# Scores of split head pairs: K and Q loaded and split once, each head on its own half of the rows

## The chip, the cores and the metric

One core of one Trainium2 chip. The metric is the device time of one launch in microseconds (us).

## The reference

Four batches, eight heads, 768 positions, head dimension 64, all float32. Sliding-window attention with sinks (window 128, 4 sink positions), then a two-layer feed-forward part over the 3072 tokens:

```python
scores = (q @ k.T) / sqrt(64)
keep = (pos_k < n_sink) | ((pos_q - pos_k >= 0) & (pos_q - pos_k < window))
a = softmax(where(keep, scores, -1e9))
x = concat_heads(a @ v)                  # 3072 x 512
h = x @ w_in                             # 512 -> 2048
out = (h * clip(h + 3, 0, 6) / 6) @ w_out
```

The matrices `w_in` and `w_out` arrive as 8-byte numbers and are turned into float32 on the chip.

## The kernel before

**Number format.** TensorE takes float32 either as it is, in two passes per product, or as `fp32r`, a shorter float that it takes in one pass. To keep accuracy in one-pass products the kernel splits an operand into a high part (rounded to `fp32r`) and a low part (the rest) and adds three or four products of parts. So every factor of the feed-forward part is a couple of tiles: `xh`/`xl`, `wih`/`wil`, `gh`/`g`, `woh`/`wol`.

**Work items.** Attention runs over 48 pairs `s`: a unit (256 positions of a batch) and two heads side by side in the 128 partitions, head 0 in rows 0 to 63 and head 1 in rows 64 to 127. Pairs 0 to 11 are plain: unsplit float32, scores by 64-row products (line 607), transposes on TensorE (712), `av` products that fill 64 columns of the array each (786). Pairs 12 to 47 are split. Of these 12 to 15 are near (a unit's first 256 positions, scores of 128 and of 256 columns), and 16 to 47 are far (scores of 272 columns in both of the two tiles `t`). Four pairs make a unit of the feed-forward part: `F` (`ffn1`, line 859, 12 products of 256 columns per half) and `G` (`ffn2`, line 892, 6 products of 512 columns per half), 12 units of 8 steps.

**Scores of a split pair, before.** `A_far` loads K and Q twice, so that each head's 64 rows stand in both halves of the partitions (tiles `kd` and `qd`, the two heads side by side in the free dimension). `B_k` makes the high part over all of `kt` and then overwrites rows 64 to 127 with the low part; `B_q` makes a full high and a full low tile. A product over 128 rows then adds two products of parts at once, so that one score tile of one head takes two products: high Q against (high K over low K), and low Q against the same. `C_score` does two heads by two products for each `t` (line 610): eight products per far pair.

**After the scores.** DVE adds the mask and takes the row minimum (620), ACT takes the exponential (637), DVE and ACT normalise, the transposed probabilities go through a buffer in device memory, POOL cuts them to shape (757), and `E_av` multiplies them with the split V (806; three or four of each head's products use 64 columns of weights, the others 128), adds the sinks (810), and DVE writes `tmp` and the split `x` (`a`, `b`, `y`, `xh`, `xl`).

**Order.** Each engine's order is fixed when the program is written. `all_tasks` lists each task with its engine, an assumed cost, what it comes after, a due number and the buffers it takes and gives; `in_order` lets time run in this model and picks for each free engine the ready task that is due first; `do` issues them in that order. On TensorE it places filler products (`keep_busy`, tile `idle`, line 357) where nothing is ready in the first `QUIET` = 34.8 us of its plan. `MARGIN` is the time a TensorE task is planned to start after a producer on another engine is done, `GIVEN` that after which a buffer counts as free. The last task of the program, `O11.1`, writes the last 128x512 result out of the accumulator in two halves, one on ACT and one on DVE.

Of the kernel before, what the change touches and what calls it, by code (L numbers as in the profile page):

```python
# [31 lines left out]
PART_DUE = (-474.72, 70.36, 106.59, 91.11, 60.03, 88.04, -112.93, 98.23, 72.34, 54.04, 219.53, 258.17, 117.07,  # L32
            108.99, 203.82, 341.65, 140.59, 151.86, 347.73, 543.5, 206.75, 263.79, 966.41, 643.54, 305.36,
            314.5, 678.08, 778.94, 385.32, 681.65, 927.6, 1439.06)
LEAD = {"kq": 204.02, "v": -124.72, "w": -805.13}
QUIET = 34.8
LATE = -387.88
SLOPE = 30.95
GLAG = 28.02
EARLY = {(0, 0): 2230.8, (0, 1): 287.72}  # L40
HOLDS = ("Pt", "pl", "qt")
KQ_HOME = {2: "kd", 3: "qd"}
MARGIN = 0.6
GIVEN = 0.25
WIRE = {"ka": 1.4, "qa": 0.9, "kq": 0.9, "v": 0.7, "w": 1.8, "bl": 0.7, "Q": 0.9, "U": 1.0, "I": 0.9, "J": 0.4}
LAND = {"w": 1.8, "ka": 1.9, "qa": 1.5, "I": 1.6, "J": 1.5, "U": 1.0, "bl": 1.6}
POOL_FREE = 7.5
BOTH = ("m", "c", "n", "kh", "kl", "qh", "ql", "vh", "vl", "bv", "zl", "xl", "wc", "wd", "wh", "wl", "h", "g")
AHEAD = {"load": -1344.45, "kt": -745.39, "v": -782.64, "S": -329.66}
ROOM = {"kq": 3, "dr": 3, "V": 2, "vr": 1, "kd": 1, "qd": 1, "kt": 1, "qt": 1, "bank": 7, "pl": 2, "Pt": 1, "ph": 2, "st": 3, "vs": 1,  # L50
# [3 lines left out]
def all_tasks():  # L54
# [10 lines left out]
    for s in range(PAIRS):  # L65
# [12 lines left out]
        else:  # L78
            hold = ("Pt",)
            add(f"ka{s}", "SP", 1.2, [], d - AHEAD["load"], ("kd",))  # L80
            add(f"qa{s}", "SP", 1.2, [], d - AHEAD["load"] + 0.1, ("qd",))
            add(f"v{s}", "SP", 0.47, [], d - AHEAD["load"] + 0.2, ("V", "vr"))
            add(f"kh{s}", "*", (0.86, 0.5) if far else (0.54, 0.336), [f"ka{s}"], d - AHEAD["kt"], ("kt",))
            add(f"kl{s}", "DVE", 0.905 if far else 0.61, [f"kh{s}"], d - AHEAD["kt"] + 0.1, (), ("kd",))
            add(f"qh{s}", "*", (0.54, 0.336), [f"qa{s}"] + [f"C{NF32 - 1}.0"] * (s == NF32), d - AHEAD["kt"] + 0.2, ("qt",))
            add(f"ql{s}", "DVE", 0.608, [f"qh{s}"], d - AHEAD["kt"] + 0.3, (), ("qd",))
            add(f"vh{s}", "*", (0.41, 0.26) if far else (0.31, 0.2), [f"v{s}"], d - AHEAD["v"])
            add(f"vl{s}", "DVE", 0.45 if far else 0.335, [f"vh{s}"], d - AHEAD["v"] + 0.1, (), ("vr",))
            add(f"C{s}.0", "PE", 0.5 if far else 0.44, [f"kl{s}", f"ql{s}"], d, ("bank", "bank", "Pt"), (), 0.35)
            add(f"C{s}.1", "PE", 0.5 if far else 0.475, [f"C{s}.0"], d + 0.05, ("bank", "bank"), ("kt", "qt"), 0.35)  # L90
# [11 lines left out]
        add(f"c{s}", "DVE", 0.41 if far else 0.2, [f"x{c}" for c in cells] if far else [f"cs{s}"], d + 0.3, lag=0.1)  # L102
# [3 lines left out]
        if far:  # L106
            add(f"T{s}", "DVE", 0.75, [f"n{c}" for c in cells], d + 0.44, ("kq",), ("Pt",))
            add(f"U{s}", "SP", 0.47, [f"T{s}"], d + 0.45, ("dr",), (f"kq@T{s}",))
            add(f"I{s}", "SP", 1.88, [f"U{s}"], d + 0.45, ("kq",), ())
            add(f"J{s}", "SP", 1.41, [f"U{s}"], d + 0.46, ("sd",), (f"dr@U{s}",))  # L110
            add(f"z{s}", "ACT", 0.265, [f"J{s}"], d + 0.62, ("pz",))
            add(f"zl{s}", "DVE", 0.34, [f"z{s}"], d + 0.62, (), ("sd",))
# [28 lines left out]
        if far:  # L141
            b = (s - 16) // 8
            before += [f"zl{s}", f"bv{b}"]
            if s % 8 == 0:
                add(f"bl{b}", "SP", 0.47, [f"c{s - 1}"], d - AHEAD["S"], ("st",) if b else ("st", "vs"))
                add(f"bs{b}", "ACT", 0.55, [f"bl{b}"] + [f"E{s - 1}.1"] * (b > 0), d)
                add(f"bv{b}", "DVE", 0.62, [f"bs{b}"], d + 0.1, (), ("st",))
        add(f"E{s}.1", "PE", 0.64 if far else 0.37, before, d + 0.7, ("bank",) * far, ("ph", "pl", "V") + ("pz",) * far, 0.3)
        add(f"a{s}.0", "*", (0.275, 0.335), [f"E{s}.1"], d + 0.8, ("tmp",))
        add(f"a{s}.1", "*", (0.275, 0.335), [f"E{s}.1", f"a{s}.0"], d + 0.8)  # L150
        add(f"b{s}.0", "DVE", 0.335, [f"a{s}.0"], d + 0.81)
        add(f"b{s}.1", "DVE", 0.335, [f"a{s}.1", f"b{s}.0"], d + 0.82, (), ("bank",))
# [15 lines left out]
    for n in range(UNITS):  # L168
# [25 lines left out]
        for t in range(2):  # L194
            half = (n, t) == (UNITS - 1, 1)
# [13 lines left out]
def in_order(tasks):  # L209
# [23 lines left out]
    while marks:  # L233
# [14 lines left out]
        while moved:  # L248
            moved = False
            for k, e in enumerate(engines):  # L250
# [65 lines left out]
def attn_ffn_kernel(ctx: ExitStack, tc: tile.TileContext, qx, kx, vx, vsx, n_sink, window, w_in, w_out, out):  # L316
# [194 lines left out]
    def A_kq(s, half=0):  # L511
# [7 lines left out]
        both = work.tile([P, 2, 400 if tag == "kd" else UT], F32, tag=tag, name="kq", bufs=3 if tag == "kq" else 1)  # L519
        kr, qr = both[:, 0, 0:UT], both[:, 1, 0:UT]  # L520
# [374 lines left out]
    def ffn_out(tt, pool, state, dst, step=None):  # L895
# [11 lines left out]
        if step != "O":  # L907
            nc.sync.dma_start(out=dst, in_=state[f"e{row}"])
# [224 lines left out]
```

## Time and profile before

| | |
|---|---|
| median of 3 runs | 683.12 us (681.72 to 683.9) |
| the profiled execution, its own time | 681.53 us |
| its span | 679.8 us, granted TensorE clock 0.998 of full speed |
| outside the span | 1.7 us |
| TensorE busy | 666.8 us |
| DVE / ACT / POOL busy | 547.4 / 436.5 / 130.7 us |

Products on TensorE are pipelined: a row's duration covers the way through the array as well, so a duration of 0.28 us can stand in a stream in which a new product starts every 0.12 us. What a product costs is read from the distance between starts. One float32 product in two passes leaves two records; one `fp32r` product leaves one.

### The profile page before, as it was taken

What the parts mean: (1) busy time and instruction counts of PE and PEld (TensorE: products, weight loads), DVE (VectorE), ACT (ScalarE), POOL (GpSimd) and SP (SyncE); (2) the same over time, 40 slices, a digit from 0 to 9 for tenths busy, and PEclk for the clock granted to TensorE, in tenths of its full rate; (3) what the DMA queues carried; (4) which work ended last, traced back from release to release, by engine and by line L of the source; (5) the groups of instructions that cost most, each with busy time, mean ns of one, the idle gap of its engine ahead of it and who ended that gap; (6) DMA issues with size and microseconds to landing.
All of it is one profiled execution on the core that took longest, in us unless ns stands there. A gap on an engine that the chain in (4) does not pass through costs nothing.

```text
span 679.8 us, 13592 instructions
## 1 busy us (share of the span) xinstructions
PE 666.8 (98%) x4522; PEld 601.5 (88%) x4522; DVE 547.4 (81%) x1383; ACT 436.5 (64%) x1118; POOL 130.7 (19%) x288
## 2 busy tenths in 40 slices
PE   9999999999999999999999999999999999999995
PEld 7779987899999989989999999999999999999994
DVE  6999997799999888889889889888998888632221
ACT  6999887667776565666576567567677566522221
POOL 2000000000223322322223224223222322400000
PEclk9999999999999999999999999999999999999999
DMA  7864573357545444354345435345545252200000
GB/s 208 258 186 153 196 227 98 109 155 189 146 123 149 109 126 147 91 148 138 108 111 156 118 99 159 107 115 157 151 113 148 83 140 73 82 1 1 31 1 35
DMA packets 82608, 84.06 MB, mean 124 GB/s; under 512 B 25572, under 2 KB 70884, under 8 KB 82532
## 3 DMA queue, kind: packets, MB, share of 16 engines
q1 hardware_dynamic: 82528, 83.14, 42.4%
q8 instruction: 37, 0.61, 0.4%
q14 instruction: 39, 0.32, 0.2%
q10 hardware_dynamic: 4, 0.00, 0.0%
HBM read 65.80 MB, written 17.30 MB: 122 GB/s over the span
## 4 chain that ended last, share of the span: by engine, by line
PE 78%; DVE 10%; ACT 4%; DMA 4%; issue 2%; SPq 1%; POOL 0%; DVEq 0%; ACTq 0%; POOLq 0%
PE hps L859 33%; PE o L892 33%; PE av L806 5%; PE sp L610 5%; DVE st L458 2%; DVE wt L461 1%; DMA st<-in_w_in_dram 1%; DVE gf L871 1%; DVE g L877 1%; DVE wol L466 1%; DMA st<-in_w_out_dram 1%; ACT Ph L637 1%; PE spt L810 1%; DVE Ph L620 1%; DMA qd<-in_qx_dram 1%
## 5 line engine op out<-in xcount | busy, mean ns | idle before, releaser
L859 PE MATMUL hps<-xh,wih 128*128 128x256 f32 x768 | 218.4, 284 | 2.9 <-DVE tmp L841 1.7
L859 PE MATMUL hps<-xh,wil 128*128 128x256 f32 x768 | 217.2, 283 | 0.0
L859 PE MATMUL hps<-xl,wih 128*128 128x256 f32 x768 | 216.4, 282 | 0.0
L859 PEld LDWEIGHTS hps<-xh,wih 128*128 128x128 f32 x768 | 144.9, 189 | 8.2 <-issue 3.1
L892 PE MATMUL o<-woh,gh 128*128 128x512 f32 x384 | 151.8, 395 | 0.0
L892 PE MATMUL o<-woh,g 128*128 128x512 f32 x384 | 151.4, 394 | 0.0
L892 PE MATMUL o<-wol,gh 128*128 128x512 f32 x384 | 151.2, 394 | 0.0
L859 PEld LDWEIGHTS hps<-xl,wih 128*128 128x128 f32 x768 | 144.8, 189 | 3.2
L859 PEld LDWEIGHTS hps<-xh,wil 128*128 128x128 f32 x768 | 144.7, 188 | 0.0
L868 ACT ACTIVATE gf<-hps,three 128x512 f32<-128x512 f32 x96 | 65.8, 686 | 87.9 <-PE hps L859 87.7
L757 POOL TENSOR_SCALAR_AFFINE_SELECT ph<-pq 128x256 fp32r<-128x256 f32 x128 | 62.9, 511 | 298.1 <-ACT pq L306 180.4
L871 DVE SCALAR_TENSOR_TENSOR gf<-gf,hps 128x512 f32<-128x512 f32 x96 | 65.6, 684 | 58.8 <-ACT gf L868 57.9
L892 PEld LDWEIGHTS o<-woh,g 128*128 128x128 f32 x384 | 72.2, 188 | 17.1
L892 PEld LDWEIGHTS o<-woh,gh 128*128 128x128 f32 x384 | 72.3, 188 | 11.7 <-issue 0.3
L892 PEld LDWEIGHTS o<-wol,gh 128*128 128x128 f32 x384 | 72.3, 188 | 11.7
L877 DVE TENSOR_TENSOR g<-gf,gh 128x512 fp32r<-128x512 f32 x96 | 68.2, 710 | 13.1 <-ACT gh L306 12.2
L306 ACT ACTIVATE gh<-gf 128x512 fp32r<-128x512 f32 x81 | 51.1, 630 | 30.9 <-DVE gf L871 28.9
L637 ACT ACTIVATE Pt<-Pt,nb 128x144 f32<-128x144 f32 (+2 forms) x144 | 59.0, 411 | 17.4 <-DVE Pt L628 16.6
L757 POOL TENSOR_SCALAR_AFFINE_SELECT pl<-pq 128x256 fp32r<-128x256 f32 x128 | 62.6, 508 | 12.0 <-DVE pq L739 11.8
L620 DVE CUSTOM_DVE_ANT_0 Pt<-sp,m_t 128x272 f32<-128x272 f32 x128 | 50.9, 436 | 3.8 <-PE sp L610 3.7
L610 PE MATMUL sp<-kt,qt 128*128 128x272 f32 (+2 forms) x288 | 43.7, 287 | 0.0
L610 PEld LDWEIGHTS sp<-kt,qt 128*128 128x128 f32 x288 | 40.0, 188 | 2.0 <-ACT Pt L637 0.2
(110 smaller groups left out, 978.3 us busy)
## 6 DMA issues: line engine op xcount, KB each, us to landing
kd<-in_kx_dram SPq DMA_DIRECT2D x64, 200.0 KB, 3.5
qd<-in_qx_dram SPq DMA_DIRECT2D x72, 128.0 KB, 3.3
dt<-tb SPq DMA_DIRECT2D x32, 288.0 KB, 2.2
st<-in_w_in_dram SPq DMA_DIRECT2D x16, 512.0 KB, 4.9
st<-in_w_out_dram SPq DMA_DIRECT2D x16, 512.0 KB, 4.6
pd<-dt SPq DMA_DIRECT2D x128, 64.0 KB, 2.1
out_dram<-ost SPq DMA_DIRECT2D x24, 256.0 KB, 2.6
vr<-in_vx_dram SPq DMA_DIRECT2D x32, 192.0 KB, 2.7
```

What stands on the lines that cost most here:

```text
L306: nc.scalar.mul(out=out, in_=src, mul=scale)
L458: nc.vector.scalar_tensor_tensor(out=low, in0=high, scalar=-2 ** 31, in1=low, op0=ALU.bitwise_and, op1=ALU.bitwise_or)
L610: nc.tensor.matmul(out=sp[g][:, 0:w], lhsT=d["qt"][:, i, g, ts], rhs=d["kt"][:, g, ks], start=(i == 0), stop=(i == 1))
L620: nc.vector.tensor_tensor_reduce(out=cell(s, g, t, 0, w), in0=sp[g][:, 0:w], in1=m[:, 0:w], scale=-SCALE, scalar=3.0e38, op0=ALU.add, op1= ...
L637: nc.scalar.activation(out=blk, in_=blk, func=AF.Exp, scale=-1.0, bias=d["nb"][:, i:i + 1], accum_out=d["sm"][:, i:i + 1])
L757: nc.gpsimd.affine_select(out=out, in_=d[f"pq{h}"][:, i].bitcast(F32), pattern=[[0, 2], [step, P]], base=0, channel_multiplier=-step, comp ...
L806: nc.tensor.matmul(out=o, lhsT=l, rhs=r, start=j == 0, stop=j == len(seq) - 1)
L859: nc.tensor.matmul(out=hp[:, half, :], lhsT=l, rhs=r, start=(j == 0 and not (early and half)), stop=(j == n - 1 and not (early and half == ...
L868: nc.scalar.activation(out=gf, in_=hp, func=AF.Relu, bias=three, scale=1.0)
L871: nc.vector.scalar_tensor_tensor(out=gf, in0=gf, scalar=6.0, in1=hp, op0=ALU.min, op1=ALU.mult)
L877: nc.vector.tensor_tensor(out=g, in0=gf, in1=gh.bitcast(F32), op=ALU.subtract)
L892: nc.tensor.matmul(out=acc, lhsT=l[:, f, ts_], rhs=r[i][:, f, :], start=(i == 0 and f == 0 and j == 0), stop=(i == NFP - 1 and f == 1 and ...
```

## The change

A split pair's K and Q are loaded once, as they lie (head 0 in rows 0 to 63, head 1 in rows 64 to 127), into one tile `kd` with two buffers; `qd` is gone. High and low parts of both are full tiles of half the former width: 400 instead of 800 columns for K, 256 instead of 512 for Q. A score tile now takes, for each head, three products over that head's 64 rows: high by high, high by low, low by high (low by low is left out). They are issued head by head, so that the products of the two heads, which use different halves of the rows of the array, follow each other as a couple: three couples per `t` in place of four products.

The planner's numbers change throughout (due numbers, leads, `KQ_HOME`, costs of the changed tasks and of some others). New in the planner is `SLACK` = 0.8: past 45 us of its plan a TensorE task is planned 0.8 us later behind a producer on another engine, and a `bank` of the accumulator counts as free 0.8 us later. The last result is written out whole, on ACT.

```diff
-EARLY = {(0, 0): 2230.8, (0, 1): 287.72}
+EARLY = {(0, 0): 1777.99, (0, 1): -175.55}
...
+SLACK = 0.8
+SETTLED = 45.0
...
-            add(f"ka{s}", "SP", 1.2, [], d - AHEAD["load"], ("kd",))
-            add(f"qa{s}", "SP", 1.2, [], d - AHEAD["load"] + 0.1, ("qd",))
+            add(f"ka{s}", "SP", 0.95, [], d - AHEAD["load"], ("kd",))
...
-            add(f"O{n}.{t}", "ACT", 0.307 if half else 0.581, [f"G{n}.7.{t}"], -50, ("st",), ("bank",))
-            if half:
-                add(f"O{n}.2", "DVE", 0.3, [f"G{n}.7.1"], -50)
-            add(f"Q{n}.{t}", "SP", 0.47, [f"O{n}.{t}"] + [f"O{n}.2"] * half, -50, (), ("st",))
+            add(f"O{n}.{t}", "ACT", 0.581, [f"G{n}.7.{t}"], -50, ("st",), ("bank",))
+            add(f"Q{n}.{t}", "SP", 0.47, [f"O{n}.{t}"], -50, (), ("st",))
...
+                slack = SLACK if now > SETTLED else 0.0
                 if gives:
-                    heapq.heappush(freed, (end + GIVEN, count, gives))
-                    heapq.heappush(marks, end + GIVEN)
+                    back = end + GIVEN + slack * ("bank" in gives)
+                    heapq.heappush(freed, (back, count, gives))
+                    heapq.heappush(marks, back)
...
-                    apart = 0.0 if tasks[nxt][0] == e else lag + MARGIN * (tasks[nxt][0] == "PE")
+                    apart = 0.0 if tasks[nxt][0] == e else lag + (MARGIN + slack) * (tasks[nxt][0] == "PE")
...
-    def A_far(s, which):
+    def A_far(s):
         b, u, p = pus[s]
-        w, src = (ncol(u), kx) if which == "k" else (UT, qx)
-        t = work.tile([P, 2, 400 if which == "k" else UT], F32, name=f"{which}d", bufs=1)
-        for half in ROWS:
-            nc.sync.dma_start(out=t[half, :, 0:w], in_=src[b, u, p, :, 0:w].rearrange("(h d) c -> d h c", h=2))
-        st_[s][f"{which}r"] = t
+        w = ncol(u)
+        t = work.tile([P, 400 + UT], F32, tag="kd", name="kd", bufs=2)
+        nc.sync.dma_start(out=t[:, 0:w], in_=kx[b, u, p, :, 0:w])
+        nc.sync.dma_start(out=t[:, 400:], in_=qx[b, u, p])
+        st_[s].update(kr=t[:, 0:w], qr=t[:, 400:])
...
-            copy_r(nc, e, d["kt"][:, :, 0:w], d["kr"][:, :, 0:w])
-        else:
-            low = d["kt"][ROWS[1], :, 0:w]
-            nc.vector.tensor_tensor(out=low, in0=d["kr"][ROWS[1], :, 0:w], in1=low.bitcast(F32), op=ALU.subtract)
+            copy_r(nc, e, d["kt"][:, 0, 0:w], d["kr"])
+        else:
+            nc.vector.tensor_tensor(out=d["kt"][:, 1, 0:w], in0=d["kr"], in1=d["kt"][:, 0, 0:w].bitcast(F32), op=ALU.subtract)
...
-            d["qt"] = work.tile([P, 2, 2, UT], F32R, name="qt", bufs=1)
+            d["qt"] = work.tile([P, 2, UT], F32R, name="qt", bufs=1)
...
-            for g in range(2):
-                if plain(s):
-                    gs = slice(D * g, D * (g + 1))
-                    nc.tensor.matmul(out=sp[g][:, 0:w], lhsT=d["qr"][gs, ts], rhs=d["kr"][gs, ks], start=True, stop=True)
-                    continue
-                for i in range(2):
-                    nc.tensor.matmul(out=sp[g][:, 0:w], lhsT=d["qt"][:, i, g, ts], rhs=d["kt"][:, g, ks],
-                                     start=(i == 0), stop=(i == 1))
+            if plain(s):
+                terms = ((d["qr"], d["kr"]),)
+            else:
+                terms = [(d["qt"][:, i], d["kt"][:, j]) for i, j in ((0, 0), (0, 1), (1, 0))]
+            for j, (l, r) in enumerate(terms):
+                for g in range(2):
+                    nc.tensor.matmul(out=sp[g][:, 0:w], lhsT=l[ROWS[g], ts], rhs=r[ROWS[g], ks],
+                                     start=j == 0, stop=j == len(terms) - 1)
```

What the planner makes of it shows in the order on TensorE, first in the middle of the program, at a far pair's scores (`sp`) with the `av` products of an earlier pair and feed-forward products (`hps`) around them. Before:

```order
L806 MATMUL av<-ph,VS 128x128
L810 MATMUL spt<-pz,vs 128x256
L610 MATMUL sp<-kt,qt 128x272 x4
L859 MATMUL hps<-xh_4332,wih_108 128x256
L859 MATMUL hps<-xl_4333,wih_108 128x256
L859 MATMUL hps<-xh_4332,wil_116 128x256
L859 MATMUL hps<-xh_4448,wih_108 128x256
```

And of the change, around the two score tiles of a far pair:

```order
L859 MATMUL hps<-xh_4868,wil_116 128x256
L610 MATMUL sp<-kt,qt 128x272 x6
L806 MATMUL av<-ph,VS 128x256
L806 MATMUL av<-ph,VS 128x128
L806 MATMUL av<-pl,VS 64x128 x2
L806 MATMUL av<-pl,VS 64x256
L806 MATMUL av<-ph,VS 128x128
L610 MATMUL sp<-kt,qt 128x272 x6
L859 MATMUL hps<-xh_4353,wih_108 128x256
```

Each score tile is six products of 64 rows instead of four of 128 rows, with products over all 128 rows ahead of them and behind them. Over the program the 36 split pairs make 52 such uninterrupted stretches of 64-row products: 20 pairs have both score tiles in one stretch, 16 have them in two.

The second place is the start of the program on TensorE, from the scores of the fourth or fifth plain pair (`sp<-kq`) to the first feed-forward products, with the filler products `idle` between. Before:

```order
L357 MATMUL idle<-rel 128x128 x2
L712 MATMUL pt<-ident_r,Ph 128x128 x6
L357 MATMUL idle<-rel 128x128
L607 MATMUL sp<-kq 128x128 x2
L607 MATMUL sp<-kq 128x256 x2
L357 MATMUL idle<-rel 128x128 x3
L786 MATMUL av<-pf,VF 64x256 x2
L786 MATMUL av<-pf,VF 64x128 x2
L357 MATMUL idle<-rel 128x128 x2
L712 MATMUL pt<-ident_r,Ph 128x128 x6
L357 MATMUL idle<-rel 128x128 x4
L859 MATMUL hps<-xh_304,wih_104 128x256
```

And of the change:

```order
L358 MATMUL idle<-rel 128x128 x4
L786 MATMUL av<-pf,VF 64x256 x2
L786 MATMUL av<-pf,VF 64x128 x2
L358 MATMUL idle<-rel 128x128 x2
L712 MATMUL pt<-ident_r,Ph 128x128 x6
L358 MATMUL idle<-rel 128x128 x2
L610 MATMUL sp<-kq 128x128 x2
L610 MATMUL sp<-kq 128x256 x2
L859 MATMUL hps<-xh_315,wih_104 128x256
L859 MATMUL hps<-xl_316,wih_104 128x256
L859 MATMUL hps<-xh_315,wil_112 128x256
L786 MATMUL av<-pf,VF 64x256 x2
```

The first feed-forward products now stand ahead of the second pair's `av` products, with 20 instead of 24 filler products ahead of them; over the whole start there are 37 filler products instead of 32.

## Rows read from the trace of the kernel before

**Rows 1.** Profile page: the span, and each engine's busy time.

```profile
span 679.8 us, 13592 instructions
PE 666.8 (98%) x4522; PEld 601.5 (88%) x4522; DVE 547.4 (81%) x1383; ACT 436.5 (64%) x1118; POOL 130.7 (19%) x288
```

**Rows 2.** Windows: stretch, length, busy of PE, PEld, DVE, ACT, POOL, clock, DMA.

```profile
34.00:68.00 34.00, 33.48 (x240) 28.29 (x239) 33.58 (x98) 33.64 (x92) 1.77 (x5) 1.00 0.56 170
306.00:340.00 34.00, 34.00 (x239) 31.33 (x239) 30.52 (x79) 20.73 (x53) 7.87 (x16) 1.00 0.44 123
```

**Rows 3.** Waits of PE, whole span: us in total, times, longest.

```profile
PE hps L859 <- DVE tmp L841: 1.7, 2, 1.2
...
PE hps L859 <- ACT pf L306: 1.2, 1, 1.2
```

**Rows 4.** Timeline of PE, a far pair's scores: start, length, instruction.

```profile
402.63 0.39 PE L892 MATMUL o<-woh,g 128*128 128x512 f32 x1
402.86 1.16 PE L610 MATMUL sp<-kt,qt 128*128 128x272 f32 x8
403.86 0.40 PE L892 MATMUL o<-woh,gh 128*128 128x512 f32 x1
```

**Rows 5.** Timeline of PE, a near pair's scores.

```profile
134.30 1.09 PE L610 MATMUL sp<-kt,qt 128*128 128x128 f32 x8
135.22 0.28 PE L859 MATMUL hps<-xh,wih 128*128 128x256 f32 x1
```

**Rows 6.** Timeline of PE, two plain pairs' 64-row scores and their neighbours.

```profile
33.09 0.82 PE L712 MATMUL pt<-ident_r,Ph 128*128 128x128 f32 x6
33.74 0.39 PE L357 MATMUL idle<-rel 128*128 128x128 f32 x2
34.06 0.49 PE L607 MATMUL sp<-kq 64*128 64x128 f32 x4
34.48 0.39 PE L859 MATMUL hps<-xh,wih 128*128 128x256 f32 x1
34.70 0.27 PE L859 MATMUL hps<-xl,wih 128*128 128x256 f32 x1
34.82 0.28 PE L859 MATMUL hps<-xh,wil 128*128 128x256 f32 x1
...
38.39 0.93 PE L607 MATMUL sp<-kq 64*128 64x128 f32 x8
39.24 0.89 PE L786 MATMUL av<-pf,VF 128*64 128x256 f32 x8
```

**Rows 7.** Timeline of PE, a far pair's products with V.

```profile
409.52 0.34 PE L806 MATMUL av<-ph,VS 128*128 128x256 f32 x2
409.69 0.40 PE L806 MATMUL av<-pl,VS 128*64 128x128 f32 x3
409.93 0.45 PE L806 MATMUL av<-ph,VS 128*128 128x128 f32 x3
...
410.69 0.40 PE L892 MATMUL o<-woh,gh 128*128 128x512 f32 x1
```

**Rows 8.** Groups by line, DVE, low parts: busy us, mean ns; then idle before.

```profile
L563 DVE TENSOR_TENSOR kt<-kd,kt 64x800 fp32r<-64x800 f32 (+1 forms) x36 | 34.8, 966 | 1.1
L571 DVE TENSOR_TENSOR qt<-qd,qt 128x512 fp32r<-128x512 f32 x36 | 25.0, 696 | 1.2 <-ACT qt L306 0.6
L554 DVE TENSOR_TENSOR VS<-vr,VS 128x384 fp32r<-128x384 f32 (+1 forms) x36 | 19.3, 537 | 0.5 <-ACT VS L306 0.4
L826 DVE TENSOR_TENSOR xl<-tmp,xh 128x256 fp32r<-128x256 f32 x36 | 16.6, 462 | 2.6 <-ACT xh L306 1.8
```

**Rows 9.** Timelines of ACT and DVE, the last results written out.

```profile
670.58 0.60 ACT L904 ACTIVATE ost<-o 128x512 f32<-128x512 f32 x1 [2.03 <-PE o L892]
671.97 0.38 ACT L904 ACTIVATE ost<-o 128x256 f32<-128x256 f32 x1 [0.80 <-PE o L892]
...
672.39 0.42 DVE L906 TENSOR_SCALAR ost<-o 128x256 f32<-128x256 f32 x1 [3.12 <-ACT ost L904]
```

More of the change, by code (lines that the diff above doesn't have):

```diff
@@ L101, in all_tasks @@
             add(f"cs{s}", "POOL", 0.22, [f"x{c}" for c in cells], d + 0.29)
-        add(f"c{s}", "DVE", 0.41 if far else 0.2, [f"x{c}" for c in cells] if far else [f"cs{s}"], d + 0.3, lag=0.1)
+        add(f"c{s}", "DVE", 0.4 if far else 0.12, [f"x{c}" for c in cells] if far else [f"cs{s}"], d + 0.3, lag=0.1)
         for c in cells:
@@ L110, in all_tasks @@
             add(f"J{s}", "SP", 1.41, [f"U{s}"], d + 0.46, ("sd",), (f"dr@U{s}",))
-            add(f"z{s}", "ACT", 0.265, [f"J{s}"], d + 0.62, ("pz",))
-            add(f"zl{s}", "DVE", 0.34, [f"z{s}"], d + 0.62, (), ("sd",))
+            add(f"z{s}", "ACT", 0.31, [f"J{s}"], d + 0.62, ("pz",))
+            add(f"zl{s}", "DVE", 0.41, [f"z{s}"], d + 0.62, (), ("sd",))
         for h in range(2):
@@ L145, in all_tasks @@
                 add(f"bl{b}", "SP", 0.47, [f"c{s - 1}"], d - AHEAD["S"], ("st",) if b else ("st", "vs"))
-                add(f"bs{b}", "ACT", 0.55, [f"bl{b}"] + [f"E{s - 1}.1"] * (b > 0), d)
+                add(f"bs{b}", "ACT", 0.64, [f"bl{b}"] + [f"E{s - 1}.1"] * (b > 0), d)
                 add(f"bv{b}", "DVE", 0.62, [f"bs{b}"], d + 0.1, (), ("st",))
         add(f"E{s}.1", "PE", 0.64 if far else 0.37, before, d + 0.7, ("bank",) * far, ("ph", "pl", "V") + ("pz",) * far, 0.3)
[L149 to L152, printed above, removed]
+        add(f"a{s}.0", "*", (0.37, 0.4), [f"E{s}.1"], d + 0.8, ("tmp",))
+        add(f"a{s}.1", "*", (0.37, 0.4), [f"E{s}.1", f"a{s}.0"], d + 0.8)
+        add(f"b{s}.0", "DVE", 0.4, [f"a{s}.0"], d + 0.81)
+        add(f"b{s}.1", "DVE", 0.4, [f"a{s}.1", f"b{s}.0"], d + 0.82, (), ("bank",))
         if far:
@@ L194, in all_tasks @@
         for t in range(2):
-            half = (n, t) == (UNITS - 1, 1)
-            add(f"O{n}.{t}", "ACT", 0.307 if half else 0.581, [f"G{n}.7.{t}"], -50, ("st",), ("bank",))
-            if half:
-                add(f"O{n}.2", "DVE", 0.3, [f"G{n}.7.1"], -50)
-            add(f"Q{n}.{t}", "SP", 0.47, [f"O{n}.{t}"] + [f"O{n}.2"] * half, -50, (), ("st",))
+            add(f"O{n}.{t}", "ACT", 0.581, [f"G{n}.7.{t}"], -50, ("st",), ("bank",))
+            add(f"Q{n}.{t}", "SP", 0.47, [f"O{n}.{t}"], -50, (), ("st",))
     return tasks
@@ L518, in A_kq @@
         tag = KQ_HOME.get(s, "kq")
-        both = work.tile([P, 2, 400 if tag == "kd" else UT], F32, tag=tag, name="kq", bufs=3 if tag == "kq" else 1)
-        kr, qr = both[:, 0, 0:UT], both[:, 1, 0:UT]
+        both = work.tile([P, 400 + UT if tag == "kd" else 2 * UT], F32, tag=tag, name="kq", bufs=3 if tag == "kq" else 2)
+        kr, qr = both[:, 0:UT], both[:, UT:2 * UT]
         cs = slice(0, UT if s else P)
@@ L895, in ffn_out @@
     def ffn_out(tt, pool, state, dst, step=None):
-        row = min(tt, 1)
         if step != "Q":
-            if f"e{row}" not in state:
-                state[f"e{row}"] = pool.tile([P, DM], F32, tag="st", name="ost", bufs=3)
-            last = step and state["n"] == UNITS - 1 and tt
-            cs = slice(256 * tt - 256, 256 * tt) if last else slice(0, DM)
-            to, src = state[f"e{row}"][:, cs], state[f"o{row}"][:, cs]
-            if tt < 2:
-                nc.scalar.mul(out=to, in_=src, mul=1.0 / 6.0)
-            else:
-                nc.vector.tensor_scalar(out=to, in0=src, scalar1=1.0 / 6.0, scalar2=None, op0=ALU.mult)
+            state[f"e{tt}"] = pool.tile([P, DM], F32, tag="st", name="ost", bufs=3)
+            nc.scalar.mul(out=state[f"e{tt}"], in_=state[f"o{tt}"], mul=1.0 / 6.0)
         if step != "O":
-            nc.sync.dma_start(out=dst, in_=state[f"e{row}"])
+            nc.sync.dma_start(out=dst, in_=state[f"e{tt}"])
     def ffn_steps(n, x, pool, psum_h, psum_o, dsts, tag=None):
@@ L951, in do @@
         elif kind in ("O", "Q"):
-            ffn_out(at[1], work, states[at[0]], dsts(at[0])[min(at[1], 1)], kind)
+            ffn_out(at[1], work, states[at[0]], dsts(at[0])[at[1]], kind)
         else:
             {"mask": lambda: masks(at[0]), "idle": lambda: keep_busy(1), "kq": lambda: A_kq(at[0]), "kb": lambda: A_kq(0, 1), "v": lambda: A_v(at[0]),
-             "ka": lambda: A_far(at[0], "k"), "qa": lambda: A_far(at[0], "q"),
+             "ka": lambda: A_far(at[0]),
              "kh": lambda: B_k(at[0], 0, on), "kl": lambda: B_k(at[0], 1), "qh": lambda: B_q(at[0], 0, on),
```

37 lines of the change are left out of this document (19 added, 18 removed).

## The prediction

> **What bounds the kernel now.** I read the page first: TensorE is busy for 666.8 of 679.8 us, DVE, the next one, for 547.4 [rows 1]. A busy share can deceive where products are pipelined, so the second view was the windows: from 306 to 340 us TensorE is busy for all 34.00 us, at full clock, and DVE (30.52) and ACT (20.73) are not; only early, from 34 to 68 us, are DVE and ACT as full (33.58 and 33.64), with the weights to convert [rows 2]. The third was the waits of TensorE: the feed-forward products waited for DVE twice, 1.7 us together, and for ACT once, 1.2 us [rows 3]; nothing larger stands there. So the time is the sum of what TensorE streams, and a term is worth what it takes or gives in starts of products there. DVE, ACT and the queues count only where they end a wait.
>
> **Edit 1: the score products (TensorE).** Before, a far pair's eight products go from 402.86 to 403.86, 0.125 us from start to start for 272 columns [rows 4]; 32 far pairs make 32.0 us. A near pair's eight take 134.30 to 135.22, 0.92 us [rows 5]: four of 128 and four of 256 columns. At the 0.12 of a 256-column product [rows 6] the latter are 0.48, which leaves 0.44, 0.11 each, for the former; four pairs make 3.7 us.
>
> After, a far pair has six couples of 64-row products. Do the two of a couple run at the same time? Rows of 64-row products there are only of plain pairs, in float32. The eight records from 38.39 to 39.24 are two heads by two passes by 128 and by 256 columns. Transposes of 128 columns start every 0.65/6 = 0.11 us (33.09 to 33.74), so a pass of 256 takes 0.22. One after the other the eight would take 4 x 0.11 + 4 x 0.22 = 1.32 us; as couples, 0.66. The row shows 0.85 [rows 6]: couples, plus 0.19 that I come to below. So I take a couple at the price of one full product: 6 x 0.125 = 0.75 us per far pair, 24.0 for 32; and 3 x 0.11 + 3 x 0.12 = 0.69 per near pair, 2.8 for four. Gain: 32.0 + 3.7 - 24.0 - 2.8 = **8.9 us**.
>
> **Edit 1, second price: changing between 128-row and 64-row products.** The order shows 52 stretches of 64-row products where there were none, each with full products on both sides. What does an entry and a leaving cost? The plain pairs give the upper bound. At 33.74 a filler product, two passes and so 0.22 at the transposes' pace, takes 0.32 before the scores start at 34.06: 0.10 more. The four records to 34.48 are two couples, 0.22, and take 0.42: 0.20 more. The first `hps` product then takes 0.22 to 34.70, the next 0.12: 0.10 more [rows 6]. That is **0.40 us per stretch**, and 52 of them would be 20.8 us, more than twice the gain. The lower bound comes from the products with V: they change between 128 and 64 columns of weights four times per far pair, in `fp32r`, and the whole stretch takes 409.52 to 410.69, 1.17 us [rows 7], for 2,304 columns (1,024 per head, 256 for the sinks), which at the pace of [rows 4] are 1.06. So four changes cost at most 0.11 us, less than a quarter of one plain stretch. The change between a two-pass and a one-pass stream isn't what costs either: transposes and fillers follow one another at 0.11 [rows 6].
>
> The two kinds of rows contradict each other, and neither is the new case: the plain rows have its shape (64 rows, two products at a time) and not its number format; the V rows have its format and a smaller shape, but fill one part of the array alone. I take the lower bound, **0**, for the forecast: what is common to all the costly rows is plain float32 in two passes, and in the one place where this kernel changes shape in the format of the new products nothing is lost. But this is the weakest choice here, and its other end is the first rival.
>
> The Trainium skill speaks against my choice: "TensorEngine Tiling (Array Packing)", section Key Properties, says that changing the tiling mode, not just the tile, drains TensorE. The plain pairs agree with it and the V products, if they count as a change of mode, do not. By the page's rule the sum would be the first rival's, by the V rows it is the forecast's.
>
> **Edit 2: half the splitting and half the loads.** DVE's low parts of K and Q take 966 and 696 ns; at half the width they are nearest to the 537 of a 384-column and the 462 of a 256-column subtraction: 0.66 us less per split pair, some 24 us over 36 pairs; ACT's high parts shrink alike, and each pair has two loads fewer in SP's queue [rows 8]. On the time I cost this at 0. TensorE covers it: where the split pairs run, it streams without a gap while DVE and ACT have idle time [rows 2]. If that cover were gone, the 24 us of DVE would be the most it could give. New behind it: K and Q share one buffer, given back only when both low parts are done, so a late `ql` now holds the next load of K too; with two such buffers that load is a pair ahead, and a wait there is in SP's queue, not on TensorE.
>
> **Edit 3: the roomier plan.** It can only take waits away from TensorE or make new ones. The two on DVE are of the kind it addresses, a TensorE task planned close behind DVE's release of an accumulator bank; at 0.55 and 1.2 us, the plan's extra 0.8 covers the one and most of the other, and DVE's shorter `kl` and `ql` stand ahead of such releases. I take **-1.7 us** [rows 3]; bounds -1.7 and, where the new order makes as many waits as it removes, 0. The wait on ACT lies at the start, where the plan has no slack.
>
> **Edit 4: the start.** Five more filler products (37 against 32), each put where the plan has nothing ready. At 0.22 us each [rows 6] that is **+1.1 us**, if they stand for time in which TensorE really has no work. Below, the 1.2 us wait for ACT before a feed-forward product may go (-1.2), since that product has moved; above, the first such product, now ahead of the second pair's `av`, may wait for its weights with all that is queued behind it: as much again as the wait of before, +2.3.
>
> **Edit 5: the last eviction.** The two halves did not run side by side: ACT's starts at 671.97, DVE's at 672.39 and ends at 672.81. A whole eviction on ACT took 0.60, so it would end at 672.57: **-0.2 us** [rows 9]; what follows (the store) is unchanged.
>
> **Sum.** -8.9 - 1.7 + 1.1 - 0.2 = -9.7 us on the profiled execution's 681.53, which is its span of 679.8 [rows 1] and 1.7 around it: 671.8. The median of the runs shown is 683.12, 1.6 above the profiled one; from it the same sum gives **673.4 us**. With the bounds of edits 3 and 4 and a couple's pace between 0.12 and 0.14 us, the forecast's own range is 669 to 679.
>
> **The rivals.**
> First, the other side: each stretch of 64-row products pays the 0.40 us of the plain ones. For it: both plain stretches of [rows 6], which have the shape of the new products. Against it: [rows 7]. Time: 20.8 us on top of the forecast, 694.2. It decides from 9.7 / 52 = 0.19 us per stretch on.
> Second, half of that, 0.20 us per stretch (the way in or the way out alone): +10.4, 683.8, so nothing gained that can be measured.
> Third, the products are as cheap as I say but the new order makes TensorE wait: accumulator banks are held longer by the plan's own account, and TensorE issues strictly in order, so a feed-forward product that waits for a bank holds all behind it. The nearest rows are the two waits of before, 0.9 us each on average [rows 3]; with one at ten of the far pairs, and those of before not removed, 9 + 1.7 us of the gain go: 684.1; with half as many, 679.6. Against it: the shorter DVE work.
>
> **How the numbers follow.** The runs of before spread over 2.2 us, so about 0.3% is what a measurement can tell from no change: below 681.1 is faster, above 685.2 slower. The forecast has 0.60; the 64-row stretches at full price 0.20; at half price 0.10; the new waits 0.10. The predicted time is the forecast's. Forecast, new waits and half price hold 0.8, from 668 to 686; the full price is left outside. Faster: 0.60 and, of new waits, 0.06; slower: 0.20, and 0.05 of the half price; the rest, 0.09, is no change.
>
> **What would show it.** Edit 1: a far pair's six couples go in 0.75 us and the product ahead and the first behind keep their 0.12 or 0.23 from start to start; if they stretch to 0.22 and 0.33, the first rival is right. The sum of starts over the score line is 27 us against 36. Edit 2: DVE busy near 523 us. Edit 3: no wait of TensorE above 0.5 us past 45 us. Edit 4: TensorE's first feed-forward product waits for a weight tile. Edit 5: the last eviction is one row of 0.60. I am wrong if the 64-row stretches cost more than 0.1 us each, if the two products of a couple don't start together (each pair then takes 1.5 us, 16 us more than now), or if TensorE has gaps where the windows now show none.

## The result and the profile after

The changed kernel took **687.31 us** (median of 4 runs, 686.86 to 687.8); the kernel before, run beside it, took 683.32 (4 runs, 681.72 to 683.9). The ratio is 1.0062, 95% interval 1.0043 to 1.0081: slower by 4.0 us. The forecast was 673.4 with a range of 668 to 686, so both the number and the side were wrong. The profiled execution of the changed kernel took 687.8 us, its span was 686.1, the granted TensorE clock 0.999. The account below goes by the profiled executions, 681.53 and 687.8 us, at granted clocks of 0.998 and 0.999; they lie 6.3 us apart where the medians lie 4.0. That goes with the clock: over the 42 runs beside the experiments the kernel before was granted 0.991 to 0.998 of full speed and took 681.4 to 683.6 us in the six runs at 0.998, 683.6 to 687.5 in the nine at 0.994 or less; the changed kernel had 0.998 or 0.999 in all four.

The profile page of the changed kernel, span, busy time and the group of the new score products:

```profile
span 686.1 us, 13698 instructions
PE 679.1 (99%) x4676; PEld 598.3 (87%) x4676; DVE 517.2 (75%) x1383; ACT 421.2 (61%) x1117; POOL 129.6 (19%) x288
...
L610 PE MATMUL sp<-kt,qt 64*128 64x272 f32 (+2 forms) x432 | 40.7, 308 | 0.0
```

Against [rows 1], DVE lost 30 us and TensorE gained 12.3. So DVE's relief, 517 where 523 was forecast, came, and the kernel is slower all the same: TensorE was the bound and still is. The windows of the changed kernel (columns as in [rows 2]) say the same of the middle of the program:

```profile
306.00:340.00 34.00, 34.00 (x248) 30.16 (x247) 26.95 (x75) 20.31 (x56) 10.54 (x23) 1.00 0.37 110
```

A TensorE that is never idle and yet takes longer must need longer for what it streams. The timeline of PE in the changed kernel, around a far pair whose two score tiles stand in one stretch, shows where:

```profile
406.35 0.28 PE L859 MATMUL hps<-xl,wih 128*128 128x256 f32 x1
406.47 0.28 PE L859 MATMUL hps<-xh,wil 128*128 128x256 f32 x1
406.68 1.02 PE L610 MATMUL sp<-kt,qt 64*128 64x272 f32 x12
407.63 0.50 PE L892 MATMUL o<-woh,gh 128*128 128x512 f32 x1
407.97 0.39 PE L892 MATMUL o<-wol,gh 128*128 128x512 f32 x1
408.20 0.39 PE L892 MATMUL o<-woh,g 128*128 128x512 f32 x1
```

Read the starts, not the durations. The feed-forward product at 406.35 keeps its 0.12 us. The next one, ahead of the scores, takes 0.21: 0.09 more. The twelve 64-row products take 0.95, where six couples at 0.125 are 0.75: so couples they are, plus 0.20. The first product behind takes 0.34, its neighbour 0.23: 0.11 more. That is 0.40 us around one stretch, the figure worked out from the plain pairs in [rows 6], at the same four places. Nothing waits for a semaphore there: this view writes a wait in brackets behind its row, as in [rows 9], and there is none.

One pair is not all 52 stretches. Summed over the trace, the products ahead of the stretches take 4.9 us more than the usual distance for their kind, the stretches themselves 37.0 us where their couples alone would be 26.8, and the first products behind 5.1 us more: 20.2 us, 0.39 per stretch.

The weight loads (PEld) at the same place show what is missing:

```profile
406.35 0.19 PEld L859 LDWEIGHTS hps<-xh,wil 128*128 128x128 f32 x1
406.68 0.80 PEld L610 LDWEIGHTS sp<-kt,qt 64*128 64x128 f32 x12
407.63 0.19 PEld L892 LDWEIGHTS o<-woh,gh 128*128 128x128 f32 x1
```

The weights of the product that starts at 406.47 begin to load at 406.35, when the product ahead of it starts; such a load is hidden. Those of the first 64-row product begin at 406.68, with the product itself, and so do those of the first full product behind, at 407.63. It is the same at all 52 entries and all 52 leavings: the load begins 1 or 2 ns ahead of its own product.

The waits of PE in the changed kernel (us in total, times, longest), all but that of the first filler product for its operand, which POOL writes (1.2 us in both kernels):

```profile
PE av L786 <- ACT pf L307: 0.3, 1, 0.3
PE hps L859 <- DVE wil L467: 0.2, 1, 0.2
PE sp L610 <- ACT pf L307: 0.2, 1, 0.2
```

The waits of [rows 3] are gone, and with them two smaller ones (0.5 and 0.2 us; a third went from 0.3 to 0.2): 3.9 us before, 0.7 now. The end of the program, in the timelines of PE and of ACT in the changed kernel:

```profile
680.72 0.40 PE L892 MATMUL o<-woh,g 128*128 128x512 f32 x1
...
681.15 0.60 ACT L898 ACTIVATE ost<-o 128x512 f32<-128x512 f32 x1 [0.81 <-PE o L892]
```

From the start of the last product to the end of the span it is 686.1 - 680.72 = 5.4 us. I call that the tail. Before, the last product started at 671.54 and the span ended at 679.8: 8.3 us. Its row before:

```profile
671.54 0.40 PE L892 MATMUL o<-woh,g 128*128 128x512 f32 x1
```

So the last product is 9.2 us later, the tail is 2.9 shorter, and the span is 6.3 longer. Two things were to be settled: what makes the stretches dear, and why the tail shrank by 2.9 us where one eviction in place of two was to give 0.2.

### The profile page after: what moved, and what is told of

Read it like the earlier page. It is cut to its first block, busy times and chain, and to the rows that moved or that the text cites. A ratio compares the mean times of both kernels' runs of the same rounds, so it can differ in the third digit from the quotient of the medians.

```text
span 686.1 us, 13698 instructions
## 1 busy us (share of the span) xinstructions
PE 679.1 (99%) x4676; PEld 598.3 (87%) x4676; DVE 517.2 (75%) x1383; ACT 421.2 (61%) x1117; POOL 129.6 (19%) x288
## 4 chain that ended last, share of the span: by engine, by line
PE 85%; DVE 10%; issue 2%; ACT 2%; DMA 1%; POOL 0%; DVEq 0%; POOLq 0%; SPq 0%; ACTq 0%
PE o L892 36%; PE hps L859 35%; PE sp L610 6%; PE av L806 5%; DVE st L459 3%; DVE wt L462 2%; DVE Ph L620 1%; DVE wol L467 1%; DMA st<-in_w_in_dram 1%; PE spt L810 1%; PE idle L358 1%; DVE gf L871 1%; DVE Ph L658 1%; DVE wil L467 1%; DVE g L877 1%
## 5 line engine op out<-in xcount | busy, mean ns | idle before, releaser
L892 PE MATMUL o<-woh,gh 128*128 128x512 f32 x384 | 154.5, 402 | 0.0
L892 PEld LDWEIGHTS o<-wol,gh 128*128 128x128 f32 x384 | 72.3, 188 | 12.3
L307 ACT ACTIVATE gh<-gf 128x512 fp32r<-128x512 f32 x85 | 53.4, 629 | 31.7 <-DVE gf L871 30.6
L307 ACT ACTIVATE kt<-kd 128x400 fp32r<-128x400 f32 (+1 forms) x35 | 18.4, 527 | 41.1 <-PE sp L610 41.1
L610 PE MATMUL sp<-kt,qt 64*128 64x272 f32 (+2 forms) x432 | 40.7, 308 | 0.0
```

Of the source, the lines that this page charges most:

```text
L307: nc.scalar.mul(out=out, in_=src, mul=scale)
L610: nc.tensor.matmul(out=sp[g][:, 0:w], lhsT=l[ROWS[g], ts], rhs=r[ROWS[g], ks], start=j == 0, stop=j == len(terms) - 1)
L892: nc.tensor.matmul(out=acc, lhsT=l[:, f, ts_], rhs=r[i][:, f, :], start=(i == 0 and f == 0 and j == 0), stop=(i == NFP - 1 and f == 1 and ...
```

## The experiments

The letters are those of the expectations. **S**: the stretches of 64-row products cost 0.40 us each at their ends, and this alone makes the kernel slower. **T**: the tail's gain comes from the whole last eviction.

**e1_before_whole_out**: the kernel before, with the last result written out whole.

```diff
-            half = (n, t) == (UNITS - 1, 1)
-            add(f"O{n}.{t}", "ACT", 0.307 if half else 0.581, [f"G{n}.7.{t}"], -50, ("st",), ("bank",))
-            if half:
-                add(f"O{n}.2", "DVE", 0.3, [f"G{n}.7.1"], -50)
...
+            add(f"O{n}.{t}", "ACT", 0.581, [f"G{n}.7.{t}"], -50, ("st",), ("bank",))
...
```

> The kernel before with one part of the change alone: the last result is written out whole on ACT. Theory T (a DVE that still has a piece of the eviction comes late to the end of the program, and the end waits for it): the time from the last product to the end of the span falls from 8.3 to about 5.4 us, so 2.9 us less, about 680.4. Rival (the forecast's step: only the eviction itself gets shorter): 0.2 us less, about 683.1, tail 8.1 us.

680.09 us (11 runs) against 683.46 (22 runs) of the kernel before: ratio 0.9965 (0.9944 to 0.9985). The timeline of PE ends with this row, the span at 677.6:

```profile
671.75 0.40 PE L889 MATMUL o<-woh,g 128*128 128x512 f32 x1
```

The last product stands where it stood (0.2 later), and the tail is 5.9 us instead of 8.3. By itself this speaks for T.

**e2_after_halves**: the changed kernel, with the two halves again (the reverse of the edit above).

> The changed kernel with the last eviction in two halves again, on ACT and DVE. Theory T: 2.9 us more than the changed kernel, about 690.2, with a tail of 8.3 us. Rival: 0.2 us more, about 687.5.

687.99 us (4 runs), 1.0079 (1.006 to 1.0099) of the kernel before. The span is 686.2, and the timelines of PE and of DVE end with:

```profile
680.21 0.40 PE L895 MATMUL o<-woh,g 128*128 128x512 f32 x1
...
681.06 0.42 DVE L909 TENSOR_SCALAR ost<-o 128x256 f32<-128x256 f32 x1 [3.15 <-ACT ost L907]
```

The tail is 6.0 us with both halves in it: 0.6 more than in the changed kernel, not 2.9. T as I had put it falls: a late half on DVE does not by itself make a tail of 8.3 us.

**e3_after_joined**: the changed kernel, with both score tiles of every split pair in one stretch, which makes 36 stretches of 52. The planner takes the joined task as one that asks for four banks, and its order on TensorE differs from the changed kernel's from 129 us on.

```diff
-            add(f"C{s}.0", "PE", 0.4 if far else 0.35, [f"kl{s}", f"ql{s}"], d, ("bank", "bank", "Pt"), (), 0.35)
-            add(f"C{s}.1", "PE", 0.39 if far else 0.37, [f"C{s}.0"], d + 0.05, ("bank", "bank"), ("kt", "qt"), 0.35)
+            add(f"C{s}", "PE", 1.19 if far else 1.12, [f"kl{s}", f"ql{s}"], d, ("bank", "bank", "bank", "bank", "Pt"), ("kt", "qt"), 0.35)
...
```

> The changed kernel with both score tiles of a split pair issued as one task, so 36 stretches of 64-row products instead of 52. Theory S (each stretch costs 0.40 us at its two ends): 16 x 0.40 = 6.4 us less than the changed kernel, about 680.9. Rival P (the ends are hidden, the new plan is what costs): nothing gained, 687 or, since the task takes four banks at once and TensorE waits for them, more.

682.92 us (10 runs), 0.9987 (0.9968 to 1.0005) of the kernel before, 4.4 less than the changed kernel. Sixteen stretches at 0.40 are 6.4. The rest is in the waits of PE, of which these come on top of those of the changed kernel:

```profile
PE av L785 <- DVE Ph L657: 0.5, 1, 0.5
PE av L805 <- ACT ph L306: 0.3, 1, 0.3
...
PE o L891 <- DVE g L876: 0.3, 1, 0.3
...
PE av L805 <- DVE pl L742: 0.3, 1, 0.3
```

They make 1.4 us of the 2.0 that are missing; the other 0.6 I could not assign to single rows. Where a stretch is avoided its price comes back, and new waits of the other order cost part of it. That the four banks make them is not shown: each of these rows waits for an operand.

**e4_full_rows**: the changed kernel in its own order, with products over all 128 rows where the 64-row products stood, four per score tile of a far pair in place of six.

```diff
-                    nc.tensor.matmul(out=sp[g][:, 0:w], lhsT=l[ROWS[g], ts], rhs=r[ROWS[g], ks],
-                                     start=j == 0, stop=j == len(terms) - 1)
+                    if plain(s):
+                        nc.tensor.matmul(out=sp[g][:, 0:w], lhsT=l[ROWS[g], ts], rhs=r[ROWS[g], ks], start=True, stop=True)
+                    elif j < 2:
+                        nc.tensor.matmul(out=sp[g][:, 0:w], lhsT=l[:, ts], rhs=r[:, ks], start=j == 0, stop=j == 1)
```

> The changed kernel in the same order, but each score tile of a split pair takes two products per head over all 128 rows (which adds the two heads together and leaves out low Q by high K, so the scores are not those of the reference) instead of three couples of 64 rows. Theory S: no 64-row stretch in the split pairs, four products of 0.125 us a tile; 47.1 us of stretches and their ends become 35.7, so 11.4 us less than the changed kernel, about 675.9. Rival P (the plan costs, not the ends): within 2 us of 687.

675.48 us (4 runs), 0.9892 (0.9874 to 0.9911) of the kernel before. The timeline of PE around one pair:

```profile
399.50 0.28 PE L861 MATMUL hps<-xh,wil 128*128 128x256 f32 x1
399.62 1.17 PE L613 MATMUL sp<-kt,qt 128*128 128x272 f32 x8
400.62 0.39 PE L894 MATMUL o<-woh,gh 128*128 128x512 f32 x1
400.85 0.39 PE L894 MATMUL o<-wol,gh 128*128 128x512 f32 x1
...
669.28 0.40 PE L894 MATMUL o<-woh,g 128*128 128x512 f32 x1
```

A third more streamed columns per pair (1.00 us instead of 0.75 of content), no ends (0.12 ahead, 0.23 behind), and the last product comes 680.72 - 669.28 = 11.4 us sooner, in the same order with the same plan. With the gain of 8.9 us that is 20.3 over 52 stretches, 0.39 each. That agrees with the 20.2 us counted in the changed kernel's own rows. S holds, and nothing else in the changed kernel is needed to make it slower.

**e5_rows_origin**: the same 64-row products, all on rows 0 to 63, so that the two of a couple can't share the array. It asks whether sharing makes the ends dear or (S1 of the expectation) the 64-row shape itself.

```diff
-                    nc.tensor.matmul(out=sp[g][:, 0:w], lhsT=l[ROWS[g], ts], rhs=r[ROWS[g], ks],
+                    nc.tensor.matmul(out=sp[g][:, 0:w], lhsT=l[ROWS[g if plain(s) else 0], ts], rhs=r[ROWS[g if plain(s) else 0], ks],
```

> The changed kernel with both heads' score products of the split pairs on rows 0 to 63 (head 1 takes head 0's data, so its scores are not those of the reference). The two products of a couple then cannot run at once: 24 + 3 us of products more. Theory S1 (a change between 128-row and 64-row products costs by itself, whichever rows are used): the product ahead of a stretch and the first behind keep their extra 0.09 and 0.10 us, 0.4 us a stretch, time about 714. Rival S2 (it costs because two products share the array): no extra at the ends, about 21 us less, 693.

713.36 us (one run). The timeline of PE around one pair:

```profile
421.77 0.28 PE L859 MATMUL hps<-xh,wil 128*128 128x256 f32 x1
421.98 1.77 PE L610 MATMUL sp<-kt,qt 64*128 64x272 f32 x12
423.68 0.50 PE L892 MATMUL o<-woh,gh 128*128 128x512 f32 x1
424.01 0.39 PE L892 MATMUL o<-wol,gh 128*128 128x512 f32 x1
```

Twelve products one after the other at 0.125 are 1.50 us; the row takes 1.70, again 0.20 more, with 0.21 ahead and 0.33 behind. So two products at a time are not the reason: products of 64 rows between products of 128 rows pay, in `fp32r` as in float32. What inside TensorE takes the time is not shown beyond the loads that do not run ahead.

**e6_v_low_f32**: why, then, did the V products of [rows 7] pay nothing? They were the row on which I had staked the lower bound. Here is the kernel before with the low parts of these products in plain float32; same shape, same place, other format (F: the format decides).

```diff
-            low = [(VS[:, slot, vhi], pl[:, c:c + o1 - o0], acc[0:D, o0:o1]) for slot, c, o0, o1 in ops]
+            low = [(VS[:, slot, vhi].bitcast(F32), pl[:, c:c + o1 - o0].bitcast(F32), acc[0:D, o0:o1]) for slot, c, o0, o1 in ops]
```

> The kernel before, with the 64-column products of V's high part and the low probabilities of the split pairs in plain float32 (two passes at half the rate: 0.47 us of stream per far pair become 1.9, some 46 us more in all). Theory F (a change of shape costs in plain float32 and not in fp32r): each of the four changes per far pair now shows 0.1 to 0.2 us extra at the product ahead and behind, time about 750 or above. Rival G (64 columns that begin at column 0 need no change in either format): starts follow one another at the stream's pace, time about 729.

747.4 us (one run). The timeline of PE, the same piece as [rows 7]:

```profile
453.14 0.34 PE L806 MATMUL av<-ph,VS 128*128 128x256 f32 x2
453.41 1.08 PE L806 MATMUL av<-pl,VS 128*64 128x128 f32 x6
454.42 0.56 PE L806 MATMUL av<-ph,VS 128*128 128x128 f32 x3
454.91 1.08 PE L806 MATMUL av<-pl,VS 128*64 128x128 f32 x6
455.92 0.33 PE L806 MATMUL av<-ph,VS 128*128 128x128 f32 x1
456.09 0.33 PE L810 MATMUL spt<-pz,vs 128*128 128x256 f32 x1
456.26 0.40 PE L892 MATMUL o<-woh,gh 128*128 128x512 f32 x1
```

The rows of the kernel before that [rows 7] leaves out:

```profile
410.22 0.40 PE L806 MATMUL av<-pl,VS 128*64 128x128 f32 x3
410.46 0.22 PE L806 MATMUL av<-ph,VS 128*128 128x128 f32 x1
410.52 0.33 PE L810 MATMUL spt<-pz,vs 128*128 128x256 f32 x1
```

Now the ends are there. The two high products ahead take 0.27 us (0.17 in [rows 7]), the three between the two low groups 0.49 (0.29), the single one behind 0.17 (0.06): 0.10 at each of four ends. A low group, four passes of 128 and two of 256 columns, takes 1.01, where the plain pace (0.11 and 0.22) gives 0.88: another 0.13 in each. All of it went to 3.12 us from 1.17, of which the second passes are 2 x (0.88 - 0.24) = 1.28 and the changes the other 0.67. So `fp32r` products with 64 columns of weights in the array's first columns run between full ones as if nothing changed, and the same shape in float32 does not.

The edit changes the format at each end as well as keeping the shape, so the change of format alone is a rival. The trace of the kernel before has it between full products, float32 transposes among `fp32r` products:

```profile
37.16 0.28 PE L859 MATMUL hps<-xh,wil 128*128 128x256 f32 x1
37.28 0.82 PE L712 MATMUL pt<-ident_r,Ph 128*128 128x128 f32 x6
37.86 0.36 PE L859 MATMUL hps<-xh,wih 128*128 128x256 f32 x1
38.06 0.28 PE L859 MATMUL hps<-xl,wih 128*128 128x256 f32 x1
```

The product ahead keeps its 0.12 us, and the six transposes with the first product behind take 0.78, where 6 x 0.11 and 0.12 are 0.78: nothing extra. In e6, then, the cost needs both, the shape and the format. The V rows were no evidence on products of 64 rows.

**e7_before_slack_whole**: the kernel before, with the planner's `SLACK` and the whole eviction, and its old due numbers.

```diff
+SLACK = 0.8
+SETTLED = 45.0
...
+                    back = end + GIVEN + slack * ("bank" in gives)
...
+                    apart = 0.0 if tasks[nxt][0] == e else lag + (MARGIN + slack) * (tasks[nxt][0] == "PE")
```

> The kernel before with the whole last eviction and with the planner's slack of 0.8 us, its due numbers and costs as they were. If slack takes away the waits of TensorE past 45 us (3.0 us in the kernel with the whole eviction alone): about 677. Rival (the new order makes as many waits elsewhere): 680 or more.

686.96 us (5 runs), 1.0065 (1.0042 to 1.0088) of the kernel before, and 6.9 above e1, from which it differs by the slack alone. The waits of PE, the longest:

```profile
PE hps L860 <- ACT pf L307: 2.1, 1, 2.1
PE hps L860 <- DVE xl L827: 1.3, 1, 1.3
...
PE av L787 <- ACT pf L307: 1.2, 1, 1.2
PE o L893 <- ACT gh L307: 1.1, 1, 1.1
```

All its waits but the first filler's are 8.5 us, in e1 5.0. Of the 3.5 more, 1.8 lie ahead of 45 us, where the slack does not act and both kernels have the same order on TensorE (up to 47.9 us); past 45 us it is 4.9 against 3.2. So slack with the old due numbers takes no waits away and the kernel is slower with it; more than 3 us of the 6.9 are in no wait, and I can't say where they come from.

**e8_plan_full_rows**: the changed kernel's planner numbers, slack and whole eviction, with loads, splitting and score products (and their costs and buffers in the plan) as before.

```diff
-KQ_HOME = {2: "kd", 3: "kd"}
+KQ_HOME = {2: "kd", 3: "qd"}
...
-            add(f"C{s}.0", "PE", 0.4 if far else 0.35, [f"kl{s}", f"ql{s}"], d, ("bank", "bank", "Pt"), (), 0.35)
+            add(f"C{s}.0", "PE", 0.5 if far else 0.44, [f"kl{s}", f"ql{s}"], d, ("bank", "bank", "Pt"), (), 0.35)
```

> The scores, loads and splitting of the kernel before (128-row products, no 64-row stretch in the split pairs) under the changed kernel's planner, due numbers and whole last eviction. Theory S: as the run of full rows on the changed kernel, about 675.5, since what DVE and ACT do more is hidden. Rival D (the 24 us of DVE work that come back end waits of TensorE again): waits of 2 to 4 us, about 678 to 680.

679.48 us (6 runs), 0.9939 (0.9922 to 0.9957) of the kernel before. The last product starts at 672.71, 1.2 us later than before, and the tail is 6.1. The waits of PE are of another kind than those of the changed kernel:

```profile
PE hps L860 <- DVE wil L467: 1.4, 2, 0.8
...
PE pt L713 <- DVE gf L872: 0.8, 1, 0.8
PE av L787 <- ACT pf L307: 0.6, 2, 0.4
```

The rival D of the expectation came true. Against e4, which streams its scores at the same pace but has the short splitting, the last product is 3.4 us later (669.28 there), and the waits without the first filler's are 3.9 us against 0.5: with the full splitting work the numbers don't fit as well. On the profiled executions (680.5 against 681.53) what is gained against before lies in the tail; of the medians' 4.1 us that is not shown.

**e9_mixed_plan**: e8 with the due numbers of the weights (`PART_DUE`), the leads and the numbers of the first feed-forward steps (`EARLY`) of the kernel before.

```diff
-EARLY = {(0, 0): 1777.99, (0, 1): -175.55}
+EARLY = {(0, 0): 2230.8, (0, 1): 287.72}
...
```

> The kernel before with the whole last eviction, the planner's slack and costs of the change and its due numbers for everything but the weights and the first feed-forward steps, which keep those of before. If the waits between 34 and 102 us in the run with all of the new numbers came from the weights' new due numbers: those 3 us go, about 676.5. Rival: the old numbers for the weights clash with the rest, waits of 3 us or more, 680 or above.

680.16 us (5 runs), 0.9941 (0.991 to 0.9972) of the kernel before: not to be told from e8 or e1, and the hoped-for 676.5 did not come. The waits of e8 for weights are gone, and waits took other places (1.4, 1.0 and 0.8 us before the transposes `pt`).

**e10_dve_shift**: the kernel before, with a constant's memset done twelve times on DVE at the start. The end of the program is the same instruction by instruction, both halves included; only DVE's program is eleven instructions longer.

```diff
-    nc.vector.memset(three, 3.0)
+    for _ in range(12):
+        nc.vector.memset(three, 3.0)
```

> The kernel before, halves of the last eviction kept, with 11 more small writes to a constant at the start of DVE's program, so that all that follows stands 11 instructions later there. If the 8.3 us from the last product to the end hang on where DVE's end of program lies in the blocks in which its instructions are fetched: a tail of about 6 us, as in the changed kernel with halves, where DVE's program is 11 rows longer. Rival T (a DVE that is late with its half is what costs): 8.3 us again. The 11 writes themselves are under 1 us and DVE waits there anyway.

681.01 us (one run). The span is 679.3, the timelines of PE and of DVE end with:

```profile
673.28 0.40 PE L893 MATMUL o<-woh,g 128*128 128x512 f32 x1
...
674.13 0.42 DVE L907 TENSOR_SCALAR ost<-o 128x256 f32<-128x256 f32 x1 [3.12 <-ACT ost L905]
```

The tail is 6.0 us, not 8.3, with the same last evictions at the same distances (the DVE half starts 0.85 us behind the last product in both). The last product comes 1.7 us later (the waits are 5.4 us against 3.9), so the run as a whole gains only 0.5.

The trace holds rows that the views leave out, the semaphores and the closing drain of each engine. Counted from the start of the last product, DVE's last semaphore row ends at 5.09 us in the kernel before and its drain begins at 7.40; the end of the span follows 0.9 us behind that. In e6, whose DVE program is that of before, it is 5.09 and 7.41, and the tail is 8.3 as well. In e10 it is 5.02 and 5.11, in e2 5.00 and 5.09. So the 2.3 us are a gap between two neighbouring instructions of DVE, which comes and goes with the length of DVE's program. It costs time only where DVE is last: e3 has such a gap too, from 0.84 to 3.38, but DVE has no half to write there, SP and ACT close after 4.5, and the tail is 5.4. Theory T thus holds for the kernel before, where the half makes DVE late and the gap comes on top; of e1's gain, 2.3 us are owed to this accident. The gap is read from one profile of each kernel. What DVE does in it is not shown, and that stays open.

## Why the prediction was wrong

**Edit 1, the products: right.** A couple costs what one full product costs: 0.95 - 0.20 us over six couples in the changed kernel, 1.50 for twelve single ones in e5. The gain of 8.9 us was there.

**Edit 1, second price: the step that failed.** The prediction had both ends, 0.40 us per stretch and 0, and said: "I take the lower bound, **0**, for the forecast". The stretch costs 0.40 at its four places, 20.2 us in all by the changed kernel's rows and 20.3 by e4. The reason given, "what is common to all the costly rows is plain float32 in two passes", was a coincidence: e5 and the changed kernel itself pay in `fp32r`. The counter-evidence, [rows 7], had the other shape, 64 columns and not 64 rows, and e6 shows that this shape is free in `fp32r` only. Nor could the transposes and fillers of [rows 6] rule out the change of format, as the prediction has it: both stand in float32, and only the rows beside e6 show that change. A row with the new products' own geometry and another format was set aside for a row with their format and another geometry. From the profile of before alone the first rival deserved at least half the chance; it got 0.20.

The Trainium skill's sentence in "TensorEngine Tiling (Array Packing)", section Key Properties, that a change of tiling mode drains TensorE, speaks of the 64-row stretches here, and the trace agrees as far as it goes: 0.40 us per stretch, and no weight load that runs ahead across its ends; a drain itself has no row in the middle of the program. For 64 columns in `fp32r` the trace shows no such cost (at most 0.11 us for four changes, [rows 7]), in float32 it does (0.67 per pair, e6).

**Why not 694.2.** The first rival had the mechanism and its price, and stood 7 us too high. About 5 of these come from the rest of the sum, which it took from the forecast; the other 2 from the medians, since the forecast set out from one that lay 1.6 above the profiled execution, and the changed kernel's lies 0.5 below its own. On the profiled executions, from 681.53 to 687.8, +6.3: the stretches net of the gain, +11.4 (e4); five more fillers, +1.1 as forecast (the distances from a filler row to the next row, summed over the start, grow from 11.4 to 12.6 us without the wait); the waits, -3.2 (3.9 to 0.7), of which the forecast had 1.7 and its bounds another 1.2 at the start; the tail, -2.9 where -0.2 was forecast. That makes +6.4. The forecast's own range adds up to 670 to 679 from its terms, not 669; nothing hangs on it.

**Edits 2 to 5.** Edit 2: half right. The relief is as large as forecast, but its 0 took it as hidden wherever TensorE streams, and e8 against e4 shows 3.4 us of waits that come back under the new plan with the full work (and with the loads and buffers of before). Edit 3: right in size, past 45 us the waits went from 2.4 to 0.7 us and none is above 0.3; e7 and e8 show that this is the plan and the shorter DVE work fitted together, not the slack alone. Edit 4: the fillers as forecast, and the wait for ACT of [rows 3] gone, the lower bound of that term; the feared wait for a weight tile did not appear (the longest is 0.2). Edit 5: the last eviction is one row of 0.60 us as forecast; the halves cost 0.6 (e2), and 2.3 came from the gap in DVE's program, which the prediction could not know from [rows 9] (e10). Neither the half price nor new waits, the other two rivals, occurred.

**What beats both kernels.** e8 at 679.48, e1 at 680.09 and e9 at 680.16 us, whose intervals overlap. e4's 675.48 is no such version, since it adds the two heads together and leaves out one of the three products of parts.

## What to carry to other kernels

Before 64-row products are put between full ones, count the stretches: here each paid 0.40 us at its ends, as much as three full products, and a couple saved 0.25/6 = 0.04 us, so that by these numbers a stretch must hold ten couples before it earns its ends (an estimate; no run has such a stretch); these held three or six. When two rows of a trace contradict each other, believe the one with the same geometry over the one with the same format, or price both ends at even chances. And when only part of a change is bad, run the rest of it alone: the plan and the shorter splitting together were worth 3 us of waits, which the stretches hid.

## What the runs showed of the hardware

Products with 64 columns of weights run between full ones at 0.11 us or less for four changes in `fp32r` ([rows 7]) and pay 0.10 us at each end and 0.13 inside in float32 (e6), while a change between full `fp32r` products and float32 transposes costs nothing that shows (0.78 us of 0.78, before); products of 64 rows pay in both formats, whether or not two of them share the array (0.20 inside in the changed kernel and in e5). At those ends the weights of the next product begin to load only 1 or 2 ns ahead of it, at all 104 places. Eleven memsets more in DVE's program took a gap of 2.3 us out of its last instructions and the tail from 8.3 to 6.0 us (e10).
